# Two pairs of PSUM banks by turns for the columns of h, and a form for at most 64 rows, in the expert stage of an attention and two-MoE kernel

## The chip, the cores and the metric

One core of a Trainium2 chip runs the whole program. The metric is the device time of one execution in microseconds; lower is better. TensorE multiplies and transposes, VectorE (DVE) and ScalarE (ACT) read its results out of PSUM, GpSimd (POOL) issues the indirect transfers that gather and scatter rows, and SyncE (SP) issues the loads of weights.

## The reference

Attention (batch 4, 12 heads, 448 positions, head size 64) with normed queries and keys gives 1792 rows of 768. A dense layer with squared ReLU (768 to 2048 to 768) follows, and then a mixture of eight experts, which is the part that the change touches:

```python
logits = x @ w_gate
e_idx = np.argmax(logits, axis=1)
gate_w = probs[np.arange(N), e_idx]              # softmax of the logits
eom = 1.0 / (1.0 + np.exp(-(x @ w_output_gate)))
for e in range(E):                               # E = 8, w1 [8, 768, 1024], w2 [8, 1024, 768]
    mask = e_idx == e
    h = np.maximum(x[mask] @ w1[e], 0.0)
    ye = h @ w2[e]
    out[mask] = gate_w[mask, None] * eom[mask, e, None] * ye
```

How many rows an expert gets depends on the inputs; the kernel learns it when it runs.

## The kernel before

Attention and the dense layer are put in order by a planner (`Plan`, line 84), with costs and priorities. Expert 0 runs at the end of that order and in `s1` and `s2` (lines 1687 and 1702). Experts 1 to 7 are written out by hand: `group(e, n_e)` is called for one after the other (line 1746), and each engine carries out its part of this text in order.

Every fp32 factor is kept as a high and a low part in fp32r, and a product is three matmuls (high by high, high by low, low by high). `split(u, h)` makes the two parts of one half of a unit of weights: ACT copies the high part (line 1499), VectorE subtracts it from the raw weights (line 1500). A unit is 768 KB. An expert has eight: units 0 to 3 hold 256 columns of w1 each, units 4 to 7 a quarter of w2 each. Splits run two units ahead of TensorE into four buffers (`HL`). When the second half of a unit is split, `load` issues on SP the load of the unit that comes 11 later.

In units 0 to 3 (line 1581) TensorE computes two blocks of h, turned (128 columns of w1 as the stationary factor, rows of x as columns): `g1_mm` for the first 256 rows, or for 128 where the expert has no more. `g1_out` applies ReLU on ACT and takes the low part on VectorE, into `HT[f]`. The two blocks of a unit use the banks `hps[0]` and `hps[1]`, in every unit. Where the expert has more than 256 rows, the same two banks then take columns 256 to 512 (lines 1592 to 1600).

In units 4 to 7, `block(j)` multiplies the rows 128 j to 128 j + 127 of h by a quarter of w2 into one of the banks `YB` (the two `tps` and the two `yps`); every second unit scales the result into `ysg[j]`. `ysg[2]` lies in the tile `hs`. Blocks 1 to 3 stand in Ifs on the count of rows.

Behind unit 5, `turn_next(e + 1, n_n)` transposes the next expert's first 256 rows of x into `X` (`x_in`, line 1515: twelve transposes on TensorE, then four copies on ACT and four subtractions on VectorE), where needed the next 256 as well, and issues four gathers (`fetch_in`) for the expert after that. `X` is [128, 6, 2, 512]: part of the model dimension, high and low, rows. At the end of `group`, `store` scatters four blocks of rows to the output by indirect DMAs on POOL, which write only the rows that exist.

An If holds all engines' code for its block, and each engine branches by itself. On an untaken If an engine adds what its instructions there would have signalled (EVENT_SEMAPHORE in the trace), so that waits elsewhere hold.

Of the kernel before, what the change touches and what calls it, by code (L numbers as in the profile page):

```python
# [10 lines left out]
F32 = mybir.dt.float32  # L11
# [3 lines left out]
AF = mybir.ActivationFunctionType  # L15
ALU = mybir.AluOpType
# [252 lines left out]
def body(ctx, tc, q, k, v, g_q, g_k, w_in, w_out, w_gate, w_og, w1, w2, out):  # L269
    nc = tc.nc  # L270
    B, H, S, D = q.shape
    P = 128
# [4 lines left out]
    NCC = DM // P  # L277
    DFF = w_in.shape[1]
    NFC = DFF // P
    E = w_gate.shape[1]  # L280
# [19 lines left out]
    ident = consts.tile([P, P], F32, name="ident")  # L300
# [48 lines left out]
    def new(pool_, tag, n, shape, dt, name, part=None):  # L349
        ring = rings.setdefault((pool_, tag), Ring(n))  # L350

        def make():
            t = env[pool_].tile(shape, dt, tag=tag, bufs=n, name=name)
            return t if part is None else t[:part]

        bf = ring.new(make)
        bf.excl = pool_ in ("pav", "phh")
        return bf
# [555 lines left out]
    def t_prio(b, f):  # L914
        return 2e6 + b * 1e5 + f * 1e3
# [350 lines left out]
    for d in range(NCC):  # L1266
        for h in range(2):
            raw, cols, pr = new(M, "w1st", 1, [P, F // 2], F32, f"w1st{d}_{h}"), slice(h * F // 2, (h + 1) * F // 2), t_prio(1, 2 * d + h)
# [117 lines left out]
    for n in range(2):  # L1386
        for d in range(NCC):
            def mm(n=n, d=d):
# [7 lines left out]
                w=[hps_b[n]], after=[m3], kind="main_w")  # L1396
# [60 lines left out]
    for t in plan.order():  # L1457
# [3 lines left out]
    dp, xps, hps, tps, yps, xgs = (env[n] for n in ("dp", "xps", "hps", "tps", "yps", "xg"))  # L1461
    w1s = env["w1s"]
    w2hl = [x() for x in w2hl]
    xT, hs, hT = xT_s(), hs_s(), [x() for x in hT_s]
# [9 lines left out]
    UC, UF = 2 * P, HF  # L1474

    X = w1s[:, :NCC].rearrange("p d (t n) -> p d t n", t=2)
    HT = [w1s[:, NCC + f].rearrange("p (t n) -> p t n", t=2) for f in range(NCC)] + [
        t.rearrange("p (t n) -> p t n", t=2) for t in (
            xT.rearrange("p a b c -> p (a b c)")[:, :F], env["slot14"][:, :F])]
    ysg = yss + [hs[:, :DM], xgs[4]]  # L1480

    YB = [t.rearrange("p a b -> p (a b)") for t in tps] + list(yps)

    def load(u):
        e, i = 1 + u // UN, u % UN
        if e >= E:
            return
        raw = RAW[u % NRAW]
        if i < 4:
            dst, src = raw.rearrange("p (a c) -> p a c", a=NCC), w1[e, :, i * UC:(i + 1) * UC]  # L1490
        else:
            n, q_ = (i - 4) // 2, i % 2
            dst, src = raw.rearrange("p (a c) -> p a c", a=UF), w2[
                e, q_ * UF * P:(q_ + 1) * UF * P, n * NH:(n + 1) * NH]
        nc.sync.dma_start(dst, src.rearrange("(a p) c -> p a c", p=P))

    def split_as(raw, hl, h):
        to = slice(h * DM, (h + 1) * DM)
        nc.scalar.copy(hl[0][:, to], raw[:, to])  # L1499
        nc.vector.tensor_sub(hl[1][:, to], raw[:, to], hl[0][:, to].bitcast(F32))  # L1500

    def split(u, h):
        if u < (E - 1) * UN:
            split_as(RAW[u % NRAW], HL[u % NHL], h)
            if h and u:
                load(u + NRAW)

    def parts(hl, a):

        return [t.rearrange("p (a c) -> p a c", a=a) for t in hl]  # L1510

    def unit(u):
        return parts(HL[u % NHL], NCC if u % UN < 4 else UF)

    def x_in(j0, n, bank):

        ps = [xps[:, :512], bank][:n]
        for j in range(n):
            for d in range(NCC):
                to = ps[j][:, d * P:(d + 1) * P] if d < 4 else xps[:, 512 + (2 * j + d - 4) * P:512 + (2 * j + d - 3) * P]  # L1520
                nc.tensor.transpose(to, xgs[j0 + j][:, d * P:(d + 1) * P], ident)  # L1521
        ends = []
        for j in range(n):
            ends.append((X[:, :4, :, (j0 + j) * P:(j0 + j + 1) * P], ps[j].rearrange("p (d n) -> p d n", d=4)))
        for j in range(n):
            ends.append((X[:, 4:, :, (j0 + j) * P:(j0 + j + 1) * P], xps[:, 512 + 2 * j * P:512 + (2 * j + 2) * P].rearrange(
                "p (d n) -> p d n", d=2)))
        for dst, src in ends:
            nc.scalar.copy(dst[:, :, 0], src)
            nc.vector.tensor_sub(dst[:, :, 1], src, dst[:, :, 0].bitcast(F32))  # L1530

    def g1_mm(ps, w, f, c0, c1):

        for d in range(NCC):
            own = slice((f % 2) * P, (f % 2 + 1) * P)
            for i, (x, y) in enumerate(((0, 0), (1, 0), (0, 1))):
                nc.tensor.matmul(  # L1537
                    ps[:, c0:c1], w[y][:, d, own], X[:, d, x, c0:c1],
                    start=d == 0 and i == 0, stop=d == NCC - 1 and i == 2)

    def g1_out(ps, f, c0, c1):
        nc.scalar.activation(HT[f][:, 0, c0:c1], ps[:, c0:c1], AF.Relu)  # L1542
        nc.vector.scalar_tensor_tensor(  # L1543
            HT[f][:, 1, c0:c1], ps[:, c0:c1], 0.0, HT[f][:, 0, c0:c1].bitcast(F32), op0=ALU.max, op1=ALU.subtract)
# [19 lines left out]
    def count_of(e):  # L1564
        return nc.values_load(cnt[0:1, 0, e:e + 1], min_val=0, max_val=NTOK)

    NG = 4

    def turn_next(e, n_e):

        x_in(0, 2, hps[0])
        with tc.If(n_e > 2 * P):
            x_in(2, 2, hps[1])
        if e + 1 < E:
            for j in range(NG):
                fetch_in(e + 1, j, j)

    def group(e, n_e):

        u0 = (e - 1) * UN  # L1580
        for i in range(4):
            w, fs = unit(u0 + i), (2 * i, 2 * i + 1)
            with tc.If(n_e > P) as cmp:  # L1583
                for f in fs:
                    g1_mm(hps[f % 2], w, f, 0, 2 * P)
            with cmp.Else():
                for f in fs:
                    g1_mm(hps[f % 2], w, f, 0, P)
            for f in fs:
                g1_out(hps[f % 2], f, 0, 2 * P)  # L1590
                split(u0 + i + 2, f % 2)
            with tc.If(n_e > 2 * P):  # L1592
                with tc.If(n_e > 3 * P) as cmp:
                    for f in fs:
                        g1_mm(hps[f % 2], w, f, 2 * P, 4 * P)
                with cmp.Else():
                    for f in fs:
                        g1_mm(hps[f % 2], w, f, 2 * P, 3 * P)
                for f in fs:
                    g1_out(hps[f % 2], f, 2 * P, 4 * P)  # L1600
        n_n = count_of(e + 1) if e + 1 < E else None
        for n in range(2):
            for q_ in range(2):
                i = 4 + 2 * n + q_
                w = unit(u0 + i)

                def block(j):
                    ps = YB[(j + 2 * n) % 4]
                    g2_mm(ps, w, q_, j)
                    if q_:  # L1610
                        g2_out(ps, n, j, tab[:, e, j])

                block(0)
                split(u0 + i + 2, 0)
                with tc.If(n_e > P):  # L1615
                    block(1)
                split(u0 + i + 2, 1)
                with tc.If(n_e > 2 * P):  # L1618
                    block(2)
                    with tc.If(n_e > 3 * P):  # L1620
                        block(3)
                if (n, q_) == (0, 1) and e + 1 < E:
                    turn_next(e + 1, n_n)
        for j in range(NG):
            store(tab[:, e, j], ysg[j])
        return n_n

    def further(e):

        nb_e = nc.values_load(cnt[0:1, 1, e:e + 1], min_val=0, max_val=NTB)  # L1630
        with tc.For_i(NG, nb_e, 1) as i:
            nc.sync.dma_start(
# [69 lines left out]
    def s2(tb, par, mid=None):  # L1702
        s2_mm(0, 0, HF)
        h_turn(1)
        s2_mm(1, 0, HF)
        if mid is not None:
            mid()
        ys, cf = yss[par], tb[:, 1:2].bitcast(F32)
        s2_mm(0, HF, NF2)
        nc.scalar.activation(ys[:, :NH], yps[0][:, :NH], AF.Copy, scale=cf)  # L1710
        s2_mm(1, HF, NF2)
        nc.vector.tensor_scalar_mul(ys[:, NH:], yps[1][:, :NH], cf)
        store(tb, ys)

    n_e = count_of(0)
    for j in range(2, NG):
        fetch(0, j, 2 + j)
# [5 lines left out]
    nc.vector.tensor_copy(tbl, tab[:, 0, 1])  # L1723
    for j in range(2, NG):
        with tc.If(n_e > j * P):
# [3 lines left out]
    n_n = count_of(1)  # L1729

    def over():

        turn_next(1, n_n)
        for h in range(2):
            split(0, h)

    s2(tbl, 0, mid=over)

    HL += [[slot(i, [P, 2 * DM], F32R, f"hl{i}")() for i in (k_, k_ + 1)] for k_ in (4, 6, 8)]
    RAW += [slot(i, [P, 2 * DM], F32, f"raw{i}")() for i in (10, 11, 13)]  # L1740
# [4 lines left out]
    for e in range(1, E):  # L1745
        n_n = group(e, n_n)

    most = nc.values_load(cnt[0:1, 2, 0:1], min_val=0, max_val=NTOK)  # L1748
    with tc.If(most > NG * P):
        for e in range(E):  # L1750
# [30 lines left out]
```

## Time and profile before

| | us |
|---|---|
| runs timed: lowest, median, highest | 1311.51, 1316.65, 1316.97 |
| the profiled execution's own time | 1307.86 |
| its span, first to last instruction | 1305.9 |
| TensorE busy in the span | 1179.5 |

The profile is one execution. Times in rows are microseconds from the start of its span, single durations nanoseconds where a column says so. A row of the timeline gives start, length, engine, line, operation, what it writes and reads, the shapes and how many instructions are merged; in brackets stands how long the engine had been idle before, and whose signal ended that. A name such as DVEq is that engine's sequencer (branches and signals). PEclk is the clock granted to TensorE as a share of 2.4 GHz. Experts 1 to 7 run from about 900 to 1284.

### The profile page before, as it was taken

What the parts mean: (1) busy time and instruction counts of PE and PEld (TensorE: products, weight loads), DVE (VectorE), ACT (ScalarE), POOL (GpSimd) and SP (SyncE); (2) the same over time, 40 slices, a digit from 0 to 9 for tenths busy, and PEclk for the clock granted to TensorE, in tenths of its full rate; (3) what the DMA queues carried; (4) which work ended last, traced back from release to release, by engine and by line L of the source; (5) the groups of instructions that cost most, each with busy time, mean ns of one, the idle gap of its engine ahead of it and who ended that gap; (6) DMA issues with size and microseconds to landing.
All of it is one profiled execution on the core that took longest, in us unless ns stands there. A gap on an engine that the chain in (4) does not pass through costs nothing. (4 is left out here: it accounts for less than half of the span.)

```text
span 1305.9 us, 19631 instructions
## 1 busy us (share of the span) xinstructions
PE 1179.5 (90%) x6752; PEld 1030.3 (79%) x6752; DVE 764.0 (58%) x1318; ACT 628.4 (48%) x1296; POOL 389.9 (30%) x428
## 2 busy tenths in 40 slices
PE   3999999999999999999999999998978779978872
PEld 2666787787778789999798989888977779977872
DVE  6999999788886871667743444334333344234440
ACT  4889787677776772344322213214333243334430
POOL 5548565655234313322300002322021110102001
PEclk9889999999999999999999999999986689989997
DMA  9832322233111001883332326365343543335100
GB/s 262 246 108 68 93 69 67 93 105 93 50 57 64 29 22 64 274 292 97 108 97 59 98 60 217 102 194 181 114 139 124 162 150 104 121 127 185 51 12 19
DMA packets 108851, 149.50 MB, mean 114 GB/s; under 512 B 11603, under 2 KB 100307, under 8 KB 108704
## 3 DMA queue, kind: packets, MB, share of 16 engines
q1 hardware_dynamic: 103616, 135.33, 33.6%
q0 software_dynamic: 5088, 12.27, 2.8%
q8 instruction: 85, 1.39, 0.4%
q14 instruction: 62, 0.51, 0.1%
HBM read 127.58 MB, written 32.10 MB: 122 GB/s over the span
## 5 line engine op out<-in xcount | busy, mean ns | idle before, releaser
L765 PE MATMUL hps<-x,win 128*128 128x448 f32 x1152 | 280.6, 376 | 1.0 <-ACT g L774 1.0
L1039 PE MATMUL yps<-gh,wout 128*128 128x448 f32 x1152 | 246.6, 370 | 3.2 <-ACT wout L317 2.9
L1039 PEld LDWEIGHTS yps<-gh,wout 128*128 128x128 f32 x1152 | 214.5, 189 | 23.3 <-ACT wout L317 3.2
L765 PEld LDWEIGHTS hps<-x,win 128*128 128x128 f32 x1152 | 211.3, 189 | 27.1 <-issue 11.1
L1537 PE MATMUL hps<-w1s,hl 128*128 128x256 f32 (+1 forms) x1296 | 182.5, 308 | 39.2 <-DVEq L1592 35.3
L1537 PEld LDWEIGHTS hps<-w1s,hl 128*128 128x128 f32 x1296 | 178.8, 219 | 43.5 <-issue 39.5
L667 ACT ACTIVATE p<-sps,nm 112x448 f32<-112x448 f32 x192 | 120.5, 635 | 36.8 <-DVE nm L664 35.2
L664 DVE TENSOR_REDUCE nm<-sps 112x1 f32<-112x448 f32 x192 | 111.7, 617 | 24.1 <-PE sps L649 20.3
L699 PE MATMUL av<-pT,v 112*128 112x448 f32 x356 | 117.0, 402 | 3.7 <-DVE pT L688 3.4
L688 DVE TENSOR_TENSOR pT<-pps,pT 112x448 fp32r<-112x448 f32 x178 | 105.3, 616 | 8.9 <-ACT pT L317 7.2
L317 ACT CAST pT<-pps 112x448 fp32r<-112x448 f32 x178 | 91.4, 534 | 28.8 <-PE av L699 14.7
L1500 DVE TENSOR_TENSOR hl<-raw,hl 128x768 fp32r<-128x768 f32 x72 | 68.1, 958 | 60.6 <-ACT hl L1499 45.8
L681 PE MATMUL pps<-ident,p 112*112 112x112 f32 x768 | 98.2, 263 | 5.4 <-DVE pT L688 1.8
L681 PEld LDWEIGHTS pps<-ident,p 112*112 112x112 f32 x768 | 82.7, 135 | 21.1 <-DVE pT L688 3.5
L317 ACT CAST gh<-gr 128x448 fp32r<-128x448 f32 x64 | 36.2, 565 | 126.0 <-PE yps L1039 116.1
L330 POOL TENSOR_TENSOR g<-g 128x448 f32<-128x448 f32 x57 | 55.9, 981 | 114.9 <-ACT g L774 113.1
L325 DVE TENSOR_TENSOR gh<-gr,gh 128x448 fp32r<-128x448 f32 x64 | 43.6, 681 | 65.0 <-ACT gh L317 65.0
L1559 POOL DMA_INDIRECT xg<-x1s,tab x24 | 25.1, 1047 | 185.9 <-PE xps L1521 181.0
L699 PEld LDWEIGHTS av<-pT,v 112*128 112x128 f32 x356 | 60.8, 190 | 20.9 <-DVE pT L688 7.1
L1543 DVE SCALAR_TENSOR_TENSOR w1s<-hps,w1s 128x256 fp32r<-128x256 f32 x54 | 22.9, 424 | 86.0 <-ACT w1s L1542 86.0
L1542 ACT ACTIVATE w1s<-hps 128x256 fp32r<-128x256 f32 x54 | 20.7, 383 | 106.8 <-PE hps L1537 103.8
L330 POOL TENSOR_TENSOR nrm<-raw,rstd 112x512 f32<-112x512 f32 x47 | 52.3, 1133 | 37.5 <-PE qkps L576 27.7
(413 smaller groups left out, 1845.3 us busy)
## 6 DMA issues: line engine op xcount, KB each, us to landing
raw<-in_moe_w_dram SPq DMA_DIRECT2D x36, 768.0 KB, 4.7
unit<-in_moe_w_dram SPq DMA_DIRECT2D x20, 768.0 KB, 4.8
gscr<-g SPq DMA_DIRECT2D x64, 224.0 KB, 2.0
gr<-gscr SPq DMA_DIRECT2D x64, 224.0 KB, 2.5
raw<-in_q_dram SPq DMA_DIRECT2D x24, 224.0 KB, 3.0
raw<-in_k_dram SPq DMA_DIRECT2D x24, 224.0 KB, 3.4
vr<-in_v_dram SPq DMA_DIRECT2D x24, 224.0 KB, 2.7
x1s<-row SPq DMA_DIRECT2D x16, 336.0 KB, 3.0
```

The lines of the kernel that those rows point to most:

```text
L317: (ACT, act(n, psum), lambda: nc.scalar.copy(dst(), src())),
L325: (DVE, dve(n), lambda: nc.vector.tensor_sub(dst(), a(), b())),
L330: (POOL, pool(n), lambda: nc.gpsimd.tensor_mul(dst(), a(), b())),
L664: add(DVE, dve(S), pr + 1 + j, lambda j=j: nc.vector.tensor_reduce(nm()[:, j:j + 1], sp[j]()[:CP, :S], AX.X, ALU.max, negate=True), r=[sp[ ...
L667: add(ACT, act(S, True, 2), pr + 3 + j, lambda j=j: nc.scalar.activation(pt[j](), sp[j]()[:CP, :S], AF.Exp, bias=nm()[:, j:j + 1], accum_o ...
L681: nc.tensor.transpose(tp()[:CP, c * CP:(c + 1) * CP], pts[c][j]()[:, kc * CP:(kc + 1) * CP], ident[:CP, :CP])
L688: add(DVE, dve(S), pq + 2, lambda: nc.vector.tensor_sub(ht()[:, 1], tp()[:CP, :S], ht()[:, 0].bitcast(F32)), r=[tp, (ht, 0)], w=[(ht, 1)], ...
L699: add(PE, 187, pq + 3 + x, lambda x=x: nc.tensor.matmul(a_()[:, :S], vt()[:, j, kc, :], ht()[:, x, :], start=kc == 0 and x == 0, stop=kc = ...
L765: add(PE, 188, pr + n_, lambda d=d, x=x, y=y, n_=n_: nc.tensor.matmul(ps()[:, :S], w()[:, x, d * P:(d + 1) * P], x_t[b, d]()[:, y, :], sta ...
L1039: nc.tensor.matmul(ps()[:, :S], w()[:, x, d * P:(d + 1) * P], hl()[:, y], start=f == 0 and i == 0, stop=f == NFC - 1 and i == 2)
L1500: nc.vector.tensor_sub(hl[1][:, to], raw[:, to], hl[0][:, to].bitcast(F32))
L1537: nc.tensor.matmul(ps[:, c0:c1], w[y][:, d, own], X[:, d, x, c0:c1], start=d == 0 and i == 0, stop=d == NCC - 1 and i == 2)
```

## The change

- `PAIRS` holds two pairs of banks, `hps` and the first two of `YB` (`tps`). Unit i of h uses `PAIRS[i % 2]`. To fit, the banks of `block(j)` in units 4 to 7 are taken in another order.
- The first If of a unit asks for more than 64 rows (`PH`) instead of more than 128, and now holds `g1_out` too, in both forms; the two splits of a unit stand together behind it. An expert with 65 to 128 rows computes 256 columns.
- At most 64 rows take `few_mm` and `few_turn`. `XF` is the place of the third 128 rows in the high part of `X`; there `turn_next` puts the high parts of the first 64 rows (VectorE) and their low parts (ACT) side by side. `few_mm` uses those as the stationary factor and 256 columns of w1 as the moving one, once for the high and once for the low weights: 12 matmuls a unit, h unturned, with 64 partitions from high x and 64 from low x. ACT copies the latter into `hs`, VectorE adds the former. `few_turn`, one unit later, transposes two blocks of 64 by 128 and does what `g1_out` does on 64 columns. The last `few_turn(3)` stands behind `block(0)` of unit 4, in an If of its own.
- `turn_next` is cut in two: the first 256 rows stay behind unit 5, the rest (`turn_more`: rows 256 to 511 and the gathers) goes behind unit 6. At expert 0's end, `turn_more` goes behind `s2`.

```diff
@@ -1564,40 +1564,71 @@
     def count_of(e):
         return nc.values_load(cnt[0:1, 0, e:e + 1], min_val=0, max_val=NTOK)
 
-    NG = 4
-
-    def turn_next(e, n_e):
+    NG, PH = 4, P // 2
+
+    PAIRS = [list(hps), YB[:2]]
+
+    XF = X[:, :, 0, 2 * P:3 * P]
+
+    def turn_next(e):
 
         x_in(0, 2, hps[0])
+        nc.vector.tensor_copy(XF[:, :, :PH], X[:, :, 0, :PH])
+        nc.scalar.copy(XF[:, :, PH:], X[:, :, 1, :PH])
+
+    def turn_more(e, n_e):
+
         with tc.If(n_e > 2 * P):
             x_in(2, 2, hps[1])
         if e + 1 < E:
             for j in range(NG):
                 fetch_in(e + 1, j, j)
 
+    def few_mm(i, w):
+
+        ps, cols = PAIRS[i % 2][0], slice(i * UC, (i + 1) * UC)
+        for d in range(NCC):
+            for y in range(2):
+                nc.tensor.matmul(
+                    ps[:, :UC], XF[:, d], w[y][:, d], start=d == 0 and y == 0, stop=d == NCC - 1 and y == 1)
+        nc.scalar.copy(hs[:PH, cols], ps[PH:, :UC])
+        nc.vector.tensor_add(hs[:PH, cols], ps[:PH, :UC], hs[:PH, cols])
+
+    def few_turn(i):
+        ps = PAIRS[i % 2][1]
+        for f in (2 * i, 2 * i + 1):
+            to = ps[:, (f % 2) * PH:(f % 2 + 1) * PH]
+            nc.tensor.transpose(to, hs[:PH, f * P:(f + 1) * P], ident[:PH, :PH])
+        for f in (2 * i, 2 * i + 1):
+            to = ps[:, (f % 2) * PH:(f % 2 + 1) * PH]
+            nc.scalar.activation(HT[f][:, 0, :PH], to, AF.Relu)
+            nc.vector.scalar_tensor_tensor(
+                HT[f][:, 1, :PH], to, 0.0, HT[f][:, 0, :PH].bitcast(F32), op0=ALU.max, op1=ALU.subtract)
+
     def group(e, n_e):
 
         u0 = (e - 1) * UN
         for i in range(4):
-            w, fs = unit(u0 + i), (2 * i, 2 * i + 1)
-            with tc.If(n_e > P) as cmp:
+            w, fs, banks_ = unit(u0 + i), (2 * i, 2 * i + 1), PAIRS[i % 2]
+            with tc.If(n_e > PH) as cmp:
                 for f in fs:
-                    g1_mm(hps[f % 2], w, f, 0, 2 * P)
+                    g1_mm(banks_[f % 2], w, f, 0, 2 * P)
+                    g1_out(banks_[f % 2], f, 0, 2 * P)
             with cmp.Else():
-                for f in fs:
-                    g1_mm(hps[f % 2], w, f, 0, P)
-            for f in fs:
-                g1_out(hps[f % 2], f, 0, 2 * P)
-                split(u0 + i + 2, f % 2)
+                few_mm(i, w)
+                if i:
+                    few_turn(i - 1)
+            for h in range(2):
+                split(u0 + i + 2, h)
             with tc.If(n_e > 2 * P):
                 with tc.If(n_e > 3 * P) as cmp:
                     for f in fs:
-                        g1_mm(hps[f % 2], w, f, 2 * P, 4 * P)
+                        g1_mm(banks_[f % 2], w, f, 2 * P, 4 * P)
                 with cmp.Else():
                     for f in fs:
-                        g1_mm(hps[f % 2], w, f, 2 * P, 3 * P)
+                        g1_mm(banks_[f % 2], w, f, 2 * P, 3 * P)
                 for f in fs:
-                    g1_out(hps[f % 2], f, 2 * P, 4 * P)
+                    g1_out(banks_[f % 2], f, 2 * P, 4 * P)
         n_n = count_of(e + 1) if e + 1 < E else None
         for n in range(2):
             for q_ in range(2):
@@ -1605,12 +1636,17 @@
                 w = unit(u0 + i)
 
                 def block(j):
-                    ps = YB[(j + 2 * n) % 4]
+                    ps = YB[(j + 2 - 2 * n) % 4]
                     g2_mm(ps, w, q_, j)
                     if q_:
                         g2_out(ps, n, j, tab[:, e, j])
 
                 block(0)
+                if i == 4:
+                    with tc.If(n_e > PH) as cmp:
+                        pass
+                    with cmp.Else():
+                        few_turn(3)
                 split(u0 + i + 2, 0)
                 with tc.If(n_e > P):
                     block(1)
@@ -1619,8 +1655,11 @@
                     block(2)
                     with tc.If(n_e > 3 * P):
                         block(3)
-                if (n, q_) == (0, 1) and e + 1 < E:
-                    turn_next(e + 1, n_n)
+                if e + 1 < E:
+                    if i == 5:
+                        turn_next(e + 1)
+                    elif i == 6:
+                        turn_more(e + 1, n_n)
         for j in range(NG):
             store(tab[:, e, j], ysg[j])
         return n_n
@@ -1730,11 +1769,12 @@
 
     def over():
 
-        turn_next(1, n_n)
+        turn_next(1)
         for h in range(2):
             split(0, h)
 
     s2(tbl, 0, mid=over)
+    turn_more(1, n_n)
 
     HL += [[slot(i, [P, 2 * DM], F32R, f"hl{i}")() for i in (k_, k_ + 1)] for k_ in (4, 6, 8)]
     RAW += [slot(i, [P, 2 * DM], F32, f"raw{i}")() for i in (10, 11, 13)]
```

## Rows read from the trace of the kernel before

**Rows 1.** The page, its first part: busy time and share of the span.

```profile
PE 1179.5 (90%) x6752; PEld 1030.3 (79%) x6752; DVE 764.0 (58%) x1318; ACT 628.4 (48%) x1296; POOL 389.9 (30%) x428
```

**Rows 2.** Waits of TensorE, 895 to 1290: us in total, times, longest us.

```profile
PE hps L1537 <- DVEq L1592: 35.3, 15, 2.6
PE xps L1521 <- DVE w1s L1530: 3.6, 1, 3.6
```

**Rows 3.** TensorE's timeline, experts 5, 6, 7: first matmuls of h and of y.

```profile
1141.06 4.43 PE L1537 MATMUL hps<-w1s,hl 128*128 128x256 f32 x36
...
1171.25 5.91 PE L1550 MATMUL tps<-hl,w1s 128*128 128x384 f32 x30 [0.57 <-ACT hT L1542]
...
1191.61 4.46 PE L1537 MATMUL hps<-w1s,hl 128*128 128x256 f32 x36 [0.43 <-DVE hl L1500]
...
1217.20 4.47 PE L1550 MATMUL tps<-hl,w1s 128*128 128x384 f32 x24 [0.56 <-ACT hT L1542]
...
1237.56 4.46 PE L1537 MATMUL hps<-w1s,hl 128*128 128x256 f32 x36 [0.43 <-DVE hl L1500]
...
1264.24 4.47 PE L1550 MATMUL tps<-hl,w1s 128*128 128x384 f32 x24 [0.15 <-PEq L1592]
```

**Rows 4.** Windows of TensorE: length, busy (matmuls), granted clock, DMA share, GB/s.

```profile
979.60:987.50 7.90, 7.90 (x36) 0.50 0.31 102
...
1198.40:1202.90 4.50, 4.50 (x36) 1.00 0.65 183
```

**Rows 5.** TensorE's timeline, experts 2 and 3, and the start of 4.

```profile
963.84 4.21 PE L1537 MATMUL hps<-w1s,hl 128*128 128x128 f32 x36 [0.81 <-ACTq L1620]
...
998.31 4.12 PE L1550 MATMUL tps<-hl,w1s 128*128 128x384 f32 x12 [0.55 <-ACT hT L1542]
1003.11 1.29 PE L1550 MATMUL tps<-hl,w1s 128*128 128x384 f32 x6 [0.68 <-PEq L1618]
...
1014.23 4.21 PE L1537 MATMUL hps<-w1s,hl 128*128 128x128 f32 x36 [0.99 <-ACT ysx L1555]
...
1054.56 1.29 PE L1550 MATMUL tps<-hl,w1s 128*128 128x384 f32 x6 [0.57 <-PEq L1618]
...
1062.62 0.87 PE L1521 MATMUL xps<-ident,xg 128*128 128x128 f32 x6 [3.56 <-DVE w1s L1530]
...
1071.68 34.03 PE L1537 MATMUL hps<-w1s,hl 128*128 128x256 f32 x288 [0.97 <-PEq L1618]
```

**Rows 6.** Groups by line and shape, 900 to 1306: busy us, mean ns, idle before.

```profile
L1500 DVE TENSOR_TENSOR hl<-raw,hl 128x768 fp32r<-128x768 f32 x72 | 68.1, 958 | 60.6 <-ACT hl L1499 45.8 <-ACTq L1615 6.4 <-ACTq L1592 4.7
L1499 ACT CAST hl<-raw 128x768 fp32r<-128x768 f32 x71 | 57.9, 827 | 2.4 <-ACTq L1592 1.7 <-ACTq L1572 0.3 <-ACT hT L1542 0.2
...
L1543 DVE SCALAR_TENSOR_TENSOR w1s<-hps,w1s 128x256 fp32r<-128x256 f32 x54 | 22.9, 424 | 86.0 <-ACT w1s L1542 86.0
...
L1542 ACT ACTIVATE w1s<-hps 128x256 fp32r<-128x256 f32 x54 | 20.7, 383 | 106.8 <-PE hps L1537 103.8 <-DVE hl L1500 3.0
```

**Rows 7.** POOL's timeline, first and fourth store of experts 1, 2 and 7.

```profile
959.71 1.03 POOL L1418 DMA_INDIRECT out_dram<-ysx,tab  x1 [5.89 <-ACT ysx L1555]
...
977.63 0.98 POOL L1418 DMA_INDIRECT out_dram<-xg,tab  x1 [6.59 <-DMA out_dram<-hs,tab]
...
1014.13 1.02 POOL L1418 DMA_INDIRECT out_dram<-ysx,tab  x1 [1.52 <-ACT ysx L1555]
...
1030.24 0.98 POOL L1418 DMA_INDIRECT out_dram<-xg,tab  x1 [1.90 <-ACTq L1592]
...
1282.63 0.98 POOL L1418 DMA_INDIRECT out_dram<-ysx,tab  x1 [34.40 <-ACT ysx L1555]
...
1292.92 0.98 POOL L1418 DMA_INDIRECT out_dram<-xg,tab  x1 [2.10 <-DMA out_dram<-hs,tab]
```

**Rows 8.** TensorE's timeline, second turn of x ahead of expert 1.

```profile
894.41 0.87 PE L1521 MATMUL xps<-ident,xg 128*128 128x128 f32 x6 [3.19 <-DVE w1s L1530]
```

**Rows 9.** Line 1592, TensorE's branch: duration ns min, median, max; first and last start.

```profile
L1592 PEldq COMPARE_BRANCH  x36: 65/208/2906, 902.9 to 1262.0; - x36
```

## Prediction

> **What bounds the kernel now.** I read the page first: TensorE is busy 90% of the span [rows 1], so only time in which it idles or runs at its lower clock can be won. The change touches the expert stage alone, so next come the waits of TensorE in that stretch [rows 2]: one line leads, 35.3 us in 15 waits for VectorE's sequencer at line 1592. To see what the waits are, the reader should look at the TensorE timeline of experts 5 to 7 and of 2 and 3 [rows 3, 5]: each of these five runs four units of h, with a wait between any two, which makes the 15. The reference's inputs send 254, 367, 30, 59, 467, 223, 232 and 160 rows to experts 0 to 7; that fits the trace, where only the stages that begin at 963.84 and 1014.23 run units of 128 columns alone [rows 5]. So experts 2 and 3 would take the new form, 1 and 4 go through the second half of h, and 5, 6 and 7 ("wide") have 129 to 256 rows.
>
> Why 2.33 us: unit i+1 writes the banks of unit i. Their last reader may be line 1600 in the untaken block at 1592, and VectorE arrives there only behind g1_out and two splits, two of 0.96 us each [rows 6]. Experts 1 and 4 have second-half work there and no gap: 288 matmuls in 34.03 us, 118 ns each [rows 5]. The waits cost twice. One unit of expert 6 ran 36 matmuls in 4.50 us at a granted clock of 1.00 (2.4 GHz), one of expert 2 took 7.90 us at 0.50 (1.2 GHz), after gaps [rows 4].
>
> **Wide experts.** From first h matmul to first y matmul: 30.19, 25.59 and 26.68 us, together 82.5 [rows 3]. With banks by turns, unit i+1 needs what VectorE did in unit i-1. VectorE's work for a unit, 2 x 0.42 + 2 x 0.96 = 2.8 us, is shorter than 36 matmuls, 4.25 us [rows 5, 6], so the wait has cover; were it gone, 2.33 us would return. Left are 144 x 0.118 = 17.0 us and the ends of units. A single untaken If costs 0.15 us, two in a row 0.57 to 0.68 [rows 3, 5]. The new If holds unequal numbers of signals in its two forms, so its end may stop TensorE as an untaken If does. I take 0.15 once, 0.57 three times and 0.4 for loading the next count, 19.3 in all, 58 for three. Gain 24.5, between 23 and 30.
>
> **Experts 1 and 4, and the If ahead of few_turn(3).** Where work was seamless, four unit ends in two experts may show a stop of 0 to 0.57 us, at most 4.6; I take 2.6. The added If behind block(0) can cost five experts as much, at most 2.9; I take 1.2. Loss 3.8, between 0 and 7.5.
>
> **Few rows, experts 2 and 3.** A unit had 36 matmuls of 128 columns; now 12 of 256, at 118 ns 1.4 us, at half clock 2.9, and two transposes. Added: an ACT copy (like 383 ns), a VectorE add (like 424), and g1_out on 64 columns, for which I take 0.22 us per instruction (between nothing and the 0.42 of 256 columns) [rows 6]. VectorE then needs 0.42 + 0.44 + 1.92 = 2.8 us a unit, with hand-overs 3.1: the bound of these units, since TensorE stays below.
>
> But the first ACT copy writes hs, and the store of the expert before reads hs. The four stores wait for each other: the first of expert 1 starts at 959.71, and the fourth only at 977.63, when the hs store has landed, 13.8 us after stage start; of expert 2 it is 1014.13 and 1030.24, 16 us; with idle queues, at the end, 1282.63 and 1292.92, 10.3 [rows 5, 7]. So copy(0) waits, and on ACT behind it wait the splits, their weight loads and all later h. While ACT stands no new load competes with the stores, so I put the release at 10.8 us into stage 2 (it began 4.1 us after its first store) and 12.7 into stage 3; the bounds are 1.7 (no wait, one mm) and 13.8 or 16.
>
> From the release: three VectorE passes, 9.5 us; the count and semaphores, 0.9; block(0) at half clock, 4.0 (4.12 before [rows 5]); few_turn(3) with ACT, VectorE and two branches, 1.5: in all 15.9 to unit 5. The rest of stage 2 took 11.1 us (1003.11 to 1014.23), I add 0.8 for a colder clock: 10.8 + 15.9 + 11.9 = 38.6 against 50.4, gain 11.8. In stage 3 the rest took 17.1 (1054.56 to 1071.68) [rows 5]; the wait of 3.56 before the second x_in goes [rows 2, 5], since block(0) of unit 6 now stands between: 12.7 + 15.9 + 14.3 = 42.9 against 57.4, gain 14.5. The bounds of the two together: 5 and 48.
>
> **Start of expert 1.** The wait of 3.19 before its second x_in [rows 8] goes the same way, but split(1) then stands ahead of g1_out on ACT and VectorE later than its matmuls do, which gives most of it back. I take 1, between 0 and 3.2.
>
> **What is moved and hidden.** The two XF copies for each of seven experts are 384 elements wide, between ACT's 383 ns (256) and 827 (768) [rows 6]; they lie beside units of 4 us on TensorE; without that cover they cost under 1 us each, 7 in all. The four fetches go behind unit 6 on POOL; about 1 us each, the last two wait for TensorE to pass the If there. They still come before the first store, which waits for the last unit; their rows are used one expert later. If late, they hold the stores, and so hs, by up to 2.6 us. The loads of weights go on from the splits; 11 units ahead is ample.
>
> **Sum.** 24.5 - 3.8 + 11.8 + 14.5 + 1.0 = 48 us. Against the profiled execution's own 1307.86 us that gives 1260; it ran 8.8 us below the median of the runs, 1316.65, by which it is 1269. I predict 1264, between the two.
>
> **A rule against it.** TensorE's gaps of 2.33 us come with halved clocks, and the named releaser is VectorE [rows 2, 4]. The Trainium skill, page "TensorE: Matmul & The Clock Gate", section "HAM oscillation — how this bites in real kernels", reports for a thin kernel that PSUM double buffering on top of another remedy gave no further gain. By that, the 24.5 would be nothing and the sum 23; this trace speaks against it.
>
> **Rivals.** (a) The few rows don't wait for hs, the stores being done in time. Then 9.1 and 11.0 us more are won: 68, time 1240 to 1249. Against it stand the four chained stores [rows 7].
> (b) The turns of banks don't remove the waits, because something else is tied to VectorE's arrival at the end of a unit. Then the wide experts win nothing and the sum is 23: 1285 to 1293. Against it: in experts 1 and 4 matmuls run on across VectorE's splits [rows 5].
> (c) Slower: TensorE's branch at 1592 took 208 ns in the median but 2906 once in 36 [rows 9]. If code, now longer by a second form, made each of 28 units stop for 2.9 us, that is 81 us, and 33 slower: 1341 to 1350. It decides from 48 / 28 = 1.7 us a unit. Against it: one case in 36. The Trainium skill, page "Runtime: NRT & Kernel Launch", section "Instruction fetch mechanics", says that a taken branch to code outside the fetched pages stalls on a fetch; the one long branch may be such a case.
>
> **Chances.** The forecast 0.65, (a) 0.15, (b) 0.12, (c) 0.05; 0.03 is left for a halfway (c), about the time before. The range, 1236 to 1290, takes in (a) and most of (b): it spans gains of 27 to 81 from the median, near the ends of the bounds, and leaves 2 in 10 out. Faster by over 0.5% (6.6 us, about what a measurement of this kernel can tell from none) 0.92, same 0.03, slower 0.05.
>
> **What would show it.** In the profile after: no waits of TensorE for VectorE's sequencer between units of experts 5 to 7, clock 1.00, some 19 us from first to last; in experts 2 and 3 one long idle stretch of ACT, ended by the hs store, then units of about 3 us led by VectorE; no x_in wait of 3.56. Wrong if that stretch is missing or much longer, if TensorE's ends of units exceed 0.6 us, or if experts 1 and 4 lose more than 1 us a unit.

## The result, and the profile after

The changed kernel takes 1267.73 us (median; 1266.33 to 1269.52) against 1316.81 for the kernel before: a ratio of 0.963, with a 95% interval of 0.960 to 0.967. The forecast was 1264, with a range of 1236 to 1290. The profiled execution took 1266.33 us, with a span of 1264.5.

TensorE's waits after, 880 to 1250, the longest first (us in total, times, longest):

```profile
PE hps L1601 <- DVEq L1623: 19.5, 2, 10.4
PE yps L1550 <- PEq L1646: 3.1, 5, 0.8
PE tps L1550 <- PEq L1581: 2.9, 4, 1.0
PE hps L1537 <- DVE w1s L1543: 2.7, 2, 1.7
```

The 15 waits between units [rows 2] are gone. In their place stand two long ones ahead of `few_turn`, one each in experts 2 and 3, and short stops on TensorE's own sequencer at two Ifs: the new one behind block(0) (line 1646) and that of `turn_more` (line 1581).

The timeline of TensorE in expert 5, which answers to the first two rows of [rows 3]:

```profile
1122.94 4.43 PE L1537 MATMUL hps<-w1s,hl 128*128 128x256 f32 x36
1127.69 4.53 PE L1537 MATMUL tps<-w1s,hl 128*128 128x256 f32 x36 [0.31 <-PEq L1623]
1132.64 4.50 PE L1537 MATMUL hps<-w1s,hl 128*128 128x256 f32 x36 [0.42 <-ACT w1s L1542]
1137.57 4.51 PE L1537 MATMUL tps<-w1s,hl 128*128 128x256 f32 x36 [0.42 <-ACT w1s L1542]
1142.62 2.35 PE L1550 MATMUL yps<-hl,w1s 128*128 128x384 f32 x12 [0.55 <-ACT hT L1542]
1145.74 3.81 PE L1550 MATMUL yps<-hl,w1s 128*128 128x384 f32 x18 [0.77 <-PEq L1646]
```

Every unit takes the 4.5 us of the full clock, the gaps are 0.3 to 0.4 us, and the last row shows the stop at the new If.

Expert 2 in the same view, to be read against the first rows of [rows 5]:

```profile
963.38 1.67 PE L1592 MATMUL hps<-hl,w1s 128*128 128x256 f32 x12 [0.81 <-ACTq L1656]
965.63 1.67 PE L1592 MATMUL tps<-hl,w1s 128*128 128x256 f32 x12 [0.58 <-PEq L1623]
976.35 0.47 PE L1601 MATMUL hps<-ident,hs 64*128 64x64 f32 x2 [9.06 <-DVEq L1623]
977.39 2.90 PE L1592 MATMUL hps<-hl,w1s 128*128 128x256 f32 x12 [0.57 <-DVE w1s L1605]
980.34 0.47 PE L1601 MATMUL tps<-ident,hs 64*128 64x64 f32 x2
981.89 2.90 PE L1592 MATMUL tps<-hl,w1s 128*128 128x256 f32 x12 [1.08 <-DVE w1s L1605]
984.72 0.47 PE L1601 MATMUL hps<-ident,hs 64*128 64x64 f32 x2
986.90 4.18 PE L1550 MATMUL yps<-hl,w1s 128*128 128x384 f32 x12 [1.71 <-ACT hl L1499]
991.02 0.47 PE L1601 MATMUL tps<-ident,hs 64*128 64x64 f32 x2
992.06 2.26 PE L1550 MATMUL yps<-hl,w1s 128*128 128x384 f32 x6 [0.57 <-PEq L1654]
```

Two units run without a long wait (1.67 us each, granted clock 1.00, which is 2.4 GHz), then TensorE stands for 9 us, and the same 12 matmuls then take 2.90 us (granted clock 0.50). What ended the standstill is seen on ACT (its timeline in expert 2) and on POOL (the first three of the four stores of expert 1, as in [rows 7]):

```profile
973.28 0.37 ACT L1594 COPY hs<-hps 64x256 f32<-64x256 f32 x1 [10.09 <-DMA out_dram<-hs,tab]
```

```profile
959.25 1.02 POOL L1418 DMA_INDIRECT out_dram<-ysx,tab  x1 [0.72 <-ACT ysx L1555]
964.06 1.01 POOL L1418 DMA_INDIRECT out_dram<-ysx,tab  x1 [3.79 <-DMA out_dram<-ysx,tab]
970.16 0.99 POOL L1418 DMA_INDIRECT out_dram<-hs,tab  x1 [5.09 <-DMA out_dram<-ysx,tab]
```

The copy into `hs` waits for the landing of the third store, which reads `hs`. TensorE's row names VectorE's sequencer, but that stands behind the add, which stands behind this copy.

Other rows of the same timeline on which the readings below rest, of experts 1, 3 and 4:

```profile
903.71 4.21 PE L1537 MATMUL hps<-w1s,hl 128*128 128x128 f32 x36 [1.71 <-DVE w1s L1543]
...
1005.35 1.67 PE L1592 MATMUL hps<-hl,w1s 128*128 128x256 f32 x12 [1.03 <-ACT ysx L1555]
1008.43 1.68 PE L1592 MATMUL tps<-hl,w1s 128*128 128x256 f32 x12 [1.41 <-PEq L1623]
...
1031.38 4.18 PE L1550 MATMUL yps<-hl,w1s 128*128 128x384 f32 x12 [2.04 <-PEq L1623]
...
1051.05 4.51 PE L1537 MATMUL hps<-w1s,hl 128*128 128x256 f32 x36 [0.99 <-ACT w1s L1529]
...
1086.57 2.28 PE L1550 MATMUL yps<-hl,w1s 128*128 128x384 f32 x12
```

### The profile page after: what moved, and what is told of

It reads as the page before. It is cut to its first block, busy times and chain, and to the rows that moved or that the text cites. A ratio compares the mean times of both kernels' runs of the same rounds, so it can differ in the third digit from the quotient of the medians.

```text
span 1264.5 us, 19418 instructions
## 1 busy us (share of the span) xinstructions
PE 1144.5 (91%) x6576; PEld 991.5 (78%) x6576; DVE 763.4 (60%) x1333; ACT 631.2 (50%) x1311; POOL 390.3 (31%) x428
## 5 line engine op out<-in xcount | busy, mean ns | idle before, releaser
L1500 DVE TENSOR_TENSOR hl<-raw,hl 128x768 fp32r<-128x768 f32 x72 | 66.5, 956 | 53.8 <-ACT hl L1499 45.8
L325 DVE TENSOR_TENSOR gh<-gr,gh 128x448 fp32r<-128x448 f32 x64 | 43.7, 682 | 65.0 <-ACT gh L317 64.7
L1550 PE MATMUL yps<-hl,w1s 128*128 128x384 f32 x270 | 59.3, 369 | 10.2 <-PEq L1646 3.1
L1537 PE MATMUL hps<-w1s,hl 128*128 128x256 f32 (+1 forms) x504 | 61.9, 281 | 5.9 <-DVE w1s L1543 2.7
L1537 PEld LDWEIGHTS hps<-w1s,hl 128*128 128x128 f32 x504 | 60.1, 189 | 7.7 <-issue 3.2
L1537 PE MATMUL tps<-w1s,hl 128*128 128x256 f32 (+1 forms) x504 | 61.3, 281 | 2.2 <-ACT w1s L1542 1.3
```

The lines of the kernel that those rows point to most:

```text
L1537: nc.tensor.matmul(ps[:, c0:c1], w[y][:, d, own], X[:, d, x, c0:c1], start=d == 0 and i == 0, stop=d == NCC - 1 and i == 2)
L1550: nc.tensor.matmul(ps[:, :NH], h[:, x], w[y][:, a], start=q_ == 0 and a == 0 and i == 0, stop=q_ == 1 and a == UF - 1 and i == 2)
```

## The experiments

All times are medians; ratios are against runs of the kernel before on the same chip, and have their 95% interval.

| what | us | ratio |
|---|---|---|
| the change | 1267.7 | 0.963 (0.960 to 0.967) |
| own_place: h of the few rows where no store reads | 1251.4, again 1249.9 | 0.954 (0.948 to 0.959), 0.955 (0.952 to 0.958) |
| turns_alone: before, with banks by turns | 1283.7 | 0.975 (0.968 to 0.981) |
| one_pair: the change with one pair of banks | 1315.5, again 1317.6 (one execution, one_pair_look) | 1.002 (0.998 to 1.005) |
| x_back: the change, x turned as before | 1272.7 | 0.968 (0.962 to 0.974) |
| only_256: before, always 256 columns | 1285.2 | 0.982 (0.977 to 0.987) |
| turns_256: both of these | 1246.8 | 0.952 (0.948 to 0.956) |
| own_no_if: own_place without the If behind block(0) | 1243.7, again 1245.9 | 0.950 (0.947 to 0.953), 0.951 (0.947 to 0.954) |
| turns_256_x: turns_256, x turned one unit later | 1241.0 | 0.946 (0.943 to 0.950) |

**own_place.** `few_mm` and `few_turn` keep the first 768 columns of h in `xgs[5]`, which is free after expert 0, and the last 256 where they were, beyond what the store reads.

```diff
+    def h_few(i):
+        return xgs[5][:, i * UC:(i + 1) * UC] if i < 3 else hs[:, i * UC:(i + 1) * UC]
...
-        nc.scalar.copy(hs[:PH, cols], ps[PH:, :UC])
-        nc.vector.tensor_add(hs[:PH, cols], ps[:PH, :UC], hs[:PH, cols])
+        nc.scalar.copy(h_i[:PH], ps[PH:, :UC])
+        nc.vector.tensor_add(h_i[:PH], ps[:PH, :UC], h_i[:PH])
```

> Theory: in experts 2 and 3 the first ACT copy stands 10 us still because hs is also what the store of the expert before reads, and the idle TensorE then works at half clock. With h of the few rows in a place that no store reads, both ACT waits for the store (20.9 us together) go, the units come at about 3.2 us instead of 4.4, and the time is 1238 to 1248 us. Rival: the splits and the hand-overs behind the copy are the real bound and the wait only moves; then less than 8 us are won, 1260 us or more.

It took 1251.4 us. TensorE's timeline in expert 2:

```profile
966.54 1.67 PE L1596 MATMUL hps<-hl,w1s 128*128 128x256 f32 x12 [0.81 <-ACTq L1660]
968.78 1.67 PE L1596 MATMUL tps<-hl,w1s 128*128 128x256 f32 x12 [0.58 <-ACT xg L1598]
971.37 0.33 PE L1605 MATMUL hps<-ident,xg 64*128 64x64 f32 x2 [0.92 <-DVEq L1627]
972.76 1.67 PE L1596 MATMUL hps<-hl,w1s 128*128 128x256 f32 x12 [1.06 <-ACT w1s L1608]
975.23 0.33 PE L1605 MATMUL tps<-ident,xg 64*128 64x64 f32 x2 [0.80 <-DVEq L1627]
978.25 2.69 PE L1596 MATMUL tps<-hl,w1s 128*128 128x256 f32 x12 [2.69 <-DVE hl L1500]
980.87 0.47 PE L1605 MATMUL hps<-ident,xg 64*128 64x64 f32 x2
981.90 3.90 PE L1550 MATMUL yps<-hl,w1s 128*128 128x384 f32 x12 [0.55 <-ACT w1s L1608]
```

The wait for the store is gone, and from the first matmul of h to the first of y it is 15.4 us instead of 23.5. The rival's share is there, too: the fourth unit waits 2.69 us for its split, and its matmuls take 2.69 us instead of 1.67. So the wait for the store did cost time, but 1251.4 lies outside both the 1238 to 1248 us of the theory and the 1260 or more of the rival.

The profiles show where the rest went. From the first matmul of h in expert 2 to that in expert 4, this run took 63.7 us and own_place_again 66.5, the change 87.7: 21 to 24 us less. But expert 1, whose code the edit leaves alone, took 4.8 and 5.6 us longer, from the first turn of its x to its first y. There TensorE waits 1.71 us in the first unit as it does after the change, and then the unit that took 4.21 us at a granted clock of 1.00 takes 6.72, at a granted clock of 0.59 (902.2 to 908.7):

```profile
902.11 6.72 PE L1537 MATMUL hps<-w1s,hl 128*128 128x128 f32 x36 [1.71 <-DVE w1s L1543]
```

**turns_alone.** The kernel before, with `PAIRS` and the other order of banks, and nothing else.

```diff
+    PAIRS = [list(hps), YB[:2]]
...
-                    g1_mm(hps[f % 2], w, f, 0, 2 * P)
+                    g1_mm(banks_[f % 2], w, f, 0, 2 * P)
...
-                    ps = YB[(j + 2 * n) % 4]
+                    ps = YB[(j + 2 - 2 * n) % 4]
```

> The kernel before with nothing but the two pairs of banks by turns. Theory: the waits of 2.33 us and the lower clock behind them are what cost experts 2 and 3 too, so their four units of h take about 18 us instead of 34.5 and 35.9, the wide experts about 18.2 instead of 30.2, 25.6 and 26.7; with a higher clock in the y units of experts 2 and 3 (about 5 us) the time is about 1250 us (1245 to 1258), less than with the whole change. Rival: the form for few rows is what shortens experts 2 and 3; then only the wide experts gain, 24 to 28 us, and the time is 1289 to 1293 us.

1283.7 us: between the two ranges, and neither theory nor rival. The waits are gone, but TensorE's timeline in expert 2 and its windows (length, busy, granted clock, DMA share, GB/s) show what the theory had missed:

```profile
970.17 4.21 PE L1537 MATMUL hps<-w1s,hl 128*128 128x128 f32 x36 [0.81 <-ACTq L1621]
974.83 4.24 PE L1537 MATMUL tps<-w1s,hl 128*128 128x128 f32 x36 [0.46 <-ACT w1s L1542]
979.65 6.75 PE L1537 MATMUL hps<-w1s,hl 128*128 128x128 f32 x36 [0.58 <-ACT w1s L1542]
986.97 7.91 PE L1537 MATMUL tps<-w1s,hl 128*128 128x128 f32 x36 [0.57 <-ACT w1s L1542]
```

```profile
974.80:979.10 4.30, 4.24 (x36) 1.00 0.31 68
979.70:986.40 6.70, 6.70 (x36) 0.59 0.64 213
987.00:994.90 7.90, 7.88 (x36) 0.50 0.31 103
```

With gaps of about half a microsecond, units of 128 columns that follow each other still fall to 1.2 GHz, though TensorE is busy in them all through. The four units take 25.3 us in expert 2 and 34.0 in expert 3 (34.5 and 35.9 before).

**only_256 and turns_256.** The If on 128 rows is left out and every expert computes 256 columns of h (the added ones belong to rows that are not stored), with one pair of banks and by turns.

```diff
-            with tc.If(n_e > P) as cmp:
-                for f in fs:
-                    g1_mm(hps[f % 2], w, f, 0, 2 * P)
-            with cmp.Else():
-                for f in fs:
-                    g1_mm(hps[f % 2], w, f, 0, P)
+            for f in fs:
+                g1_mm(hps[f % 2], w, f, 0, 2 * P)
```

> The kernel before with the banks by turns, and every expert computes 256 columns of h, so no unit has 128. Theory: with the waits gone, TensorE was busy 7.91 us of each later unit of experts 2 and 3 at half clock, so there the lower clock goes with the short matmuls themselves; with 256 columns the four units of these experts take about 19.8 us instead of 25.3 and 34.0, y units 2 to 5 us less, and the time is 1257 to 1264 us. Rival: the clock fell because of the stops of 0.5 to 0.8 us between units, which stay; then a unit takes 8.5 us and more, and the time is 1290 us or above.

> The kernel before with 256 columns of h in every expert and one pair of banks. Theory: in experts 2 and 3 TensorE's matmuls get the higher clock for much of the time, but the waits of 2.33 us stay: four units take 26 to 30 us instead of 34.5 and 35.9, and the time is 10 to 18 us below the kernel before; banks and columns together give more than either. Rival: with the waits the clock stays at half in these experts also with 256 columns, a unit takes 8.5 us plus 2.33, and the time is 10 us above the kernel before or more.

1246.8 and 1285.2 us: both rivals fell, and the units of h took what the theories said, but both times lie below their ranges (1257 to 1264; 10 to 18 us below the kernel before, where it was 23.5). In the windows of the first, third and fourth unit of expert 2, with the turns:

```profile
962.90:967.40 4.50, 4.50 (x36) 1.00 0.80 224
972.40:976.80 4.40, 4.40 (x36) 1.00 0.71 224
977.10:981.60 4.50, 4.47 (x36) 1.00 0.54 162
```

Twice the columns take nearly the time that the half had at the full clock (4.5 us for 4.2), and the clock stays there. With one pair, the waits are as before in number and length:

```profile
PE hps L1537 <- DVEq L1588: 35.0, 15, 2.3
```

Yet of the eight units of h in experts 2 and 3, five took 4.5 us there (1.00) and three 6.0 (0.72).

From the first matmul of h to the first of y, each figure being the difference of two starts:

| | expert 2 | expert 3 |
|---|---|---|
| before | 34.5 | 35.9 |
| turns_alone | 25.3 | 34.0 |
| only_256 | 28.6 | 27.1 |
| turns_256 | 19.3 | 19.3 |
| the change | 23.5 | 26.0 |
| own_place | 15.4 | 15.5 |

The form for few rows is the shortest of all here where it doesn't wait for the store, and with that wait it loses to plain 256 columns. But its `few_turn(3)` comes behind the end of this stretch, and the first matmuls of y that follow take 3.90 us in expert 2, against 2.35 in turns_256. Over both stages, from the first h of expert 2 to that of expert 4, it takes 63.7 and 66.5 us (own_place and its second run), turns_256_x, which also turns x later, 68.7: of a lead of 8 us in the table, 2 to 5 are left.

**one_pair.** One line differs from the change; the profile shown is of its second run, one_pair_look.

```diff
-    PAIRS = [list(hps), YB[:2]]
+    PAIRS = [list(hps), list(hps)]
```

> The changed kernel with one pair of banks in every unit. Theory: experts 5, 6 and 7 get back their waits between units, about 24 us, experts 2 and 3 a few us, since a unit's matmuls must then wait for the copy and the add of the unit before: 1290 to 1300 us. Rival: the waits went because g1_out now stands ahead of both splits and inside the If, and not because of the banks; then the time stays near 1268 us.

> A profile of the changed kernel with one pair of banks, which took as long as the kernel before. Theory: TensorE waits in each unit for VectorE's signal at the end of the untaken If, now behind both splits: nine waits of 2.8 us or more in experts 5 to 7, and every few_mm in experts 2 and 3 waits for it too, which takes back most of what the form for few rows gave. Rival: experts 5 to 7 lose little, and the whole loss sits in experts 2 and 3.

1315.5 us, as slow as the kernel before. TensorE's waits in one_pair_look:

```profile
PE hps L1592 <- DVEq L1623: 40.7, 6, 14.2
PE hps L1537 <- DVEq L1623: 28.8, 9, 3.2
```

The second expectation held; 1315.5 lies outside the 1290 to 1300 us of the first. The nine waits of experts 5 to 7 are back and are 3.20 instead of 2.33 us, since both splits now come after the second `g1_out`; every later `few_mm` waits for the same signal. The first expectation had seen the nine, but not how much experts 2 and 3 would lose. That g1_out's new place alone removes waits is refuted.

**x_back.** `turn_more` stands directly behind `turn_next` again, and in `over`.

> The changed kernel with the third and fourth block turned behind unit 5 again. Theory: the waits of TensorE for the second turn of x come back, 3.6 us ahead of expert 4 (less the 0.95 that is left now) and 3.2 ahead of expert 1 (less the 1.7 that its first unit waits now), while the stops at the If behind unit 6 (2.9 us in four places) get shorter: 1268 to 1271 us. Rival: the move is worth nothing or less, 1265 to 1268 us.

1272.7 us; the interval overlaps that of the change, so the time alone doesn't decide. The waits of TensorE do:

```profile
PE xps L1521 <- DVE w1s L1530: 6.6, 2, 3.4
```

After the change one such wait of 0.95 us is left. With the stops at line 1581 (2.9 us) taken off, the move is worth some 3 us by the waits and 5 by the medians; 1272.7 is a little above the 1268 to 1271 us expected.

**own_no_if.** `few_turn(3)` goes behind `few_turn(2)` in unit 3, and the If at line 1646 falls away.

> As with the place of its own for h, and few_turn(3) moved into unit 3, so that the If behind block(0) falls away. Theory: the five stops of 0.55 to 0.77 us (2.9 together) go, against about 1 us more in experts 2 and 3, where TensorE now waits for the last add ahead of block(0): 1 to 2 us faster than the kernel with the place of its own. Rival: the wait for the last add is longer than the stops were; no change, or 1 to 4 us slower.

> The kernel with the place of its own for h once more, beside the one without the If: 1248 to 1254 us by the theory, as before.

> The form for few rows in a place of its own and without the If, beside turns_256_x on the same chip: 1240 to 1246 us, as before.

1243.7 us beside 1249.9 for own_place, with runs that don't overlap, and 1245.9 the second time: 4 to 6 us, more than the 1 to 2 expected. The stops at the If are 2.9 and 3.1 us in the two profiles with it. The stages of the five experts concerned shrink by more: from the first y to the next expert's first h (in expert 7, to the end) each is 0.8 to 1.1 us shorter (means of two profiles), together 4.5, which covers the difference of the medians; what makes the 1.5 us beyond the stops is open. The profiles differ by some 3 us more ahead of expert 1, where the edit changes nothing. Experts 2 and 3 gave nothing that these profiles show: together 63.7 and 66.5 us with the If, 63.9 and 65.6 without.

**turns_256_x.** turns_256 with the x move of the change.

> The banks by turns, 256 columns always, and the third and fourth block turned one unit later. Theory: the waits of TensorE ahead of the second turn of x (3.66 and 3.19 us) mostly go, against longer stops behind unit 6: 3 to 5 us below the kernel without the move, 1241 to 1245 us, level with the form for few rows at its best. Rival: the move gives nothing here, 1246 us or more.

1241.0 us, level with own_no_if's 1245.9 on the same chip or slightly below, and 5.8 below turns_256, of which the intervals of the ratios overlap. It is below both kernels of the case, with 256 columns for everybody and no form of its own for few rows.

## Why the prediction was right, point by point

| term | forecast | measured in the profiles |
|---|---|---|
| experts 5 to 7, h | +24.5 | 82.5 to 58.7: +23.7 |
| expert 2 | +11.8 | 50.4 to 42.0: +8.4 |
| expert 3 | +14.5 | 57.4 to 45.7: +11.7 |
| from x's first turn to expert 1's y | +1.0 | 43.7 to 41.9: +1.8, its loss included |
| units' ends in 1 and 4, If behind block(0) | -3.8 | -1.7 in expert 4; -3.1 at the If |
| sum | 48 | 40.8; the profiled times differ by 41.5, the medians by 49.1 |

That the median came within 4 us of the forecast is in part luck. In the profiles the few rows gave 20.1 us instead of 26.3, and the whole 41.5 instead of 48. The medians differ by more because the profiled execution of the kernel before was 9 us below its median, and that of the change 1.4 below.

**Wide experts.** The step held to half a microsecond a stage: 19.7, 19.7 and 19.3 us for 19.3 (1122.94 to 1142.62, 1164.10 to 1183.84, 1205.09 to 1224.42). Rival (b) fell with turns_alone and one_pair: the waits go with the banks and come back with them. The rule cited against this step (the Trainium skill, "TensorE: Matmul & The Clock Gate", "HAM oscillation — how this bites in real kernels": in a thin kernel, no further gain from PSUM double buffering on top of another remedy) does not carry over: here a second pair alone gave a ratio of 0.975.

**The store.** The wait that would take the place of those removed was named with its place, and it is there: ACT waited 10.09 and 10.83 us for the landing of the hs store, in experts 2 and 3, and the release came 9.9 and 12.1 us into the stage (10.8 and 12.7 forecast). Rival (a) fell with it. own_place shows that it cost 16 to 18 us by the medians and 11 to 13 by the ratios, which go by runs of the kernel before on the same chip; taking the wait away was a change of a few lines.

**The term that was mis-sized: from the release to unit 5.** 15.9 us forecast, 18.8 and 19.2 measured (973.28 to 992.06, and 1017.44 to 1036.62). The step "the bound of these units, since TensorE stays below" failed. At half clock a unit on TensorE is 2.90 of matmuls, 0.47 of transposes and a stop of 1.08 behind them, 4.5 us from start to start (977.39 to 981.89), against VectorE's 3.1. I had counted the matmuls alone. The part behind block(0) came out as forecast: 5.2 us for 5.5.

**A reading that was wrong without harm.** "The waits cost twice" compared two units, and both follow a wait of 2.33 us: that of expert 6 (1198.40) at 1.00, that of expert 2 at 0.50. So these rows did not show that the gap halves the clock. In the kernel before, five of the nine units behind a wait in experts 5 to 7 took 4.5 us, and four took 5.9 to 6.0, as this window:

```profile
1147.80:1153.90 6.10, 6.01 (x36) 0.72 0.71 238
```

The nine waits were 21.3 us, of which 3.5 are left as short gaps, and the slow units cost 5.9: together the 23.7. In experts 2 and 3, to which the row of 0.50 belonged, the gaps alone are not the cause: turns_alone kept 0.50 there without the long gaps, only_256 had units at 1.00 with them, and in turns_256 all eight units were at 1.00. Had the forecast been for the turns alone, it would have been 34 us too low, as my expectation of that run was (1250 for 1283.7).

**Expert 1, a gain that other profiles don't show.** The +1.8 comes from one profile (889.75 to 933.42 before, 890.63 to 932.53 after: 43.7 and 41.9 us). Six other profiles of kernels with the later turn of x have the wait in expert 1's first unit, too (1.4 to 2.4 us), and in each the 36 matmuls behind it were granted 0.52 to 0.63: 44.8 us in turns_256_x, 46.7 to 47.5 in the others. There the term is a loss of 1 to 4 us, outside its forecast of 0 to 3.2. Why the change's own profile stayed at 1.00 is open.

**Small terms.** The If behind block(0) stopped all five experts by 0.55 to 0.77 us (3.1, not 1.2), and own_no_if puts its whole cost at 4.5. The If of `turn_more` was forgotten: behind unit 6 it adds another untaken If to those on blocks 1 to 3, 2.9 us of stops in four places, where there were about 1.4 before. Experts 1 and 4 did not stop at each unit's end; their loss was a wait in the first unit, 1.71 us in expert 1 for `g1_out` behind a split, and 1.02 in expert 4 for the second `g1_out`. Rival (c) did not come outside the few rows: there TensorE stopped at most 0.56 us at the end of a unit of h. In experts 2 and 3 its sign did show: TensorE's branch at line 1623 took 2.01, 2.31 and 2.43 us there, part of it while matmuls still ran, and behind two of these TensorE stopped 1.41 and 2.04 us, more than the 0.6 named under "What would show it". Whether these are fetches of code is not shown.

## What to carry to other kernels

An engine's wait for another's end-of-block signal is as long as all that stands ahead of the signal in that engine's order; a second set of buffers takes the wait off, and where the order is changed without it, as in one_pair, the wait only grows. A buffer borrowed for a new use brings its old readers along: before `hs` was written early in a stage, the store that read it late should have been looked up. And a form with a third of the matmuls should be tried against the plain one made uniform: two short edits (banks, 256 columns for all) gave about as much as the special form at its best (1246.8 and, with x turned later, 1241.0 us, against 1243.7 and 1245.9).

## What the runs showed that I had not expected

TensorE's matmuls with 128 columns of fp32r took as long as those with 256 at the full clock (36 in 4.21 and 4.46 us), and units of 128 that followed each other were granted 0.50 while the engine was busy 7.88 of 7.90 us, where the same units with 256 columns were granted 1.00. Why is not shown: in expert 1 after the change, units of 128 and of 256 columns followed each other without a gap and stayed at 1.00.

An If that is not taken stopped TensorE for 0.15 to 0.43 us, the If with an Else behind block(0) for 0.55 to 0.77, two in a row for 0.55 to 0.8 and three for 0.98. In the rows of the change, TensorE's sequencer gives its signal when the engine's own earlier matmuls have ended: in expert 1 they end at 934.86, the signal of line 1646 comes at 934.9, and the next matmul starts at 935.41; in expert 5 it is 1144.97, 1145.0 and 1145.74. In turns_alone TensorE also stood for 1.11 and 2.14 us in the middle of a unit with nothing to wait for in the profile. The Trainium skill ("Runtime: NRT & Kernel Launch", "Instruction fetch mechanics") describes a stall for a taken branch whose target has not been fetched; these stops lie between two matmuls of a unit, and no run here shows what they were.
